# Attention and squared-ReLU FFN in one kernel: the last 64 keys of two pairs of heads, multiplied with their values on quarters of the array

## The chip, the cores and the metric

The kernel runs on one core of a Trainium2 chip. The metric is the device time of one execution in microseconds, less being better. An execution covers the whole program, with the input and output in the chip's memory.

## The reference

Queries and keys are normalised by their root mean square and scaled by a gain; softmax attention follows; the heads are laid side by side and go through a feed-forward network whose activation is the square of a ReLU. All is float32.

```python
# q, k, v: (8, 12, 448, 64); g_q, g_k: (64,); w_in: (768, 2048); w_out: (2048, 768)
def _attn_ref(q, k, v, g_q, g_k):
    def rmsnorm(x, g):
        rms = np.sqrt(np.mean(x * x, axis=-1, keepdims=True) + 1e-06)
        return x / rms * g
    q_n, k_n = (rmsnorm(q, g_q), rmsnorm(k, g_k))
    scores = 1.0 / np.sqrt(q.shape[-1]) * np.matmul(q_n, k_n.transpose(0, 1, 3, 2))
    scores = scores - np.max(scores, axis=-1, keepdims=True)
    attn = np.exp(scores)
    attn = attn / (np.sum(attn, axis=-1, keepdims=True) + 1e-09)
    return np.matmul(attn, v)

x = attn_out.transpose(0, 2, 1, 3).reshape(8 * 448, 12 * 64)
h = np.maximum(x @ w_in, 0.0)
out = h * h @ w_out                      # (3584, 768)
```

## The kernel before

**Pairs and units.** The work of attention goes by pairs of heads: 8 batches of 6 pairs, 48 pairs, numbered i from 0. The two heads of a pair (e = 0 and 1) lie on partitions 0 to 63 and 64 to 127. The feed-forward network goes by units of two batches, 12 pairs each, so there are four units. `ffn(u)` is a Python generator that writes one product of unit u at each step; it works with Strassen-like products (seven in place of eight), whose operands are the forms `T1` to `T4` of x, the sums `S1` to `S4` of the hidden layer and the weights' forms, which are made in the first unit and kept in device memory.

**Order.** The instructions of each engine stand in the order in which the program writes them; nothing reorders them. While the FFN of one unit runs, the attention of the next unit's pairs is put between its products. Pair i is scored in visit i, and its weights meet the values in visit i + 1. `run(until)` writes FFN products up to a given cost, and then a visit is written. `tasks` and `pool_tasks` are queues of small steps for DVE, ACT and POOL that are written one at a time behind the FFN products. Pairs with `whole(i)`, i > 24, have one visit each (`visit_whole`); pairs 13 to 24 have two half visits (`visit_among`); pairs up to 12 come ahead of the FFN (`visit_alone`). So the visits of the second and third unit's pairs, 24 to 47, are with one exception whole visits, 25 to 48.

**Keys.** Of the 448 keys 384 make three slots (m = 0, 1, 2) of 128 keys. The last 64 keys of an even pair and the last 64 of the odd pair after it share one slot, m = `NJ` = 3: the even pair's on rows 0 to 63, the odd pair's on rows 64 to 127. I call two such pairs a couple. Scores stand with the keys on partitions and the 448 queries along the row.

**A whole visit i, in PE's order:**

- `score` (L397) of slots 0 and 1 of pair i: keys times queries, contracted over 64, so that the two heads run on the two halves of the array's rows; into banks 0, 1 (m=0) and 2, 3 (m=1).
- `attend` (L477) of pair i - 1, slot by slot: values times weights, into bank 4, the two heads on the two halves of the array's columns. `forget` releases the weights' tiles, and `weigh` (L405 on ACT) writes the exponentials of slots 0 and 1 of pair i between them, each into a `wT` tile (8 buffers).
- In an even visit `both_denominators` (L516) of the couple before: four 32-column products of the sums with ones, into bank 0, from where DVE's `take_sums` (L549) transposes them.
- `score` and `weigh` of the slots that are left: m=2 in an odd visit (banks 1, 2); m=2 and m=3 in an even one (banks 1, 2 and 3, 0). The m=3 products serve both pairs of the couple: 64 rows by 64 columns each, two heads by two pairs.

For slot `NJ`, `attend` multiplies the whole 128 rows of the shared weights with the tile `lasts[i % 2]`, which holds this pair's last values on its own 64 rows and zeros on the others:

```python
                nc.tensor.matmul(
                    values_bank(i)[ds(e * D, D), :],
                    lhsT=lasts[i % 2][mine, e, :] if m == NJ else values[i][:, m, e, :],
                    rhs=weights[key_of(i, m), e][mine], start=n == 0, stop=n == NJ,
                )
```

An even pair takes this slot last, in the odd visit that follows it; an odd pair takes it first, in the next even visit (`values_of`). `load_v` (L342, L347 on SP) loads a pair's values in its own visit.

**After a visit.** In an odd visit ACT copies bank 4, the even pair's unnormalised values, to its x tile (L1162). POOL adds up the weights of the slots (`add_up`, L424). After an even visit `invert_both` takes reciprocals of the couple's sums and spreads them; POOL multiplies the even pair's x by them (L535), and `finish` multiplies the odd pair's values, out of bank 4, on DVE (L582). Then the x tiles are taken into the forms (L610).

**FFN lines.** L705 is the first product (its PSUM roles are banks 5 to 7, copied by ACT at L712, made into the hidden layer on DVE at L725 and ACT at L726 and L727); POOL makes the hidden sums (L741); L757 and L786 are the second products; DVE adds them up (L827, L803), ACT in the first block (L825, L801). L651 and L656 load the weights' forms.

Of the kernel before, what the change touches and what calls it, by code (L numbers as in the profile page):

```python
# [13 lines left out]
F32 = mybir.dt.float32  # L14
# [3 lines left out]
ALU = mybir.AluOpType  # L18
# [3 lines left out]
P = 128  # L22


NJ = 3
# [198 lines left out]
def program(ctx, tc, rows, v, g, wide, ones, moe_w_in, moe_w_out, out, shift):  # L224

    nc = tc.nc

    B, H, S, D = v.shape
# [21 lines left out]
    lasts = [const.tile([P, 2, D], F32, name=f"lasts{n}") for n in range(2)]  # L250
# [7 lines left out]
    banks = [psum.tile([P, 512], F32, name=f"bank{n}") for n in range(8)]  # L258
# [4 lines left out]
    LASTS = S - NJ * P  # L263
    assert 2 * LASTS == P and LASTS == D and NPAIR % 2 == 0
    values, turned, through = {}, {}, {}
    weights, sums, inverse, xts, forms = {}, {}, {}, {}, {}
    complete = deque()


# [4 lines left out]
    def whole(i):  # L274
        return i > 2 * 2 * NPAIR

    def slots_of(i, n):

        return [m for m in (2 * n, 2 * n + 1) if m < NJ + 1 - i % 2]

    def values_of(i):

        return [NJ, 0, 1, 2] if i % 2 else [0, 1, 2, NJ]

    def key_of(i, m):
        return (i - i % 2, m) if m == NJ and not shift else (i, m)

    def alone(i):

        return pairs[i][0] < 2  # L290
# [47 lines left out]
    def load_v(i):  # L338
        b, c = pairs[i]
        values[i] = io.tile([P, NJ, 2, D], F32, name="vt", tag="vt")  # L340
        for e in range(2):
            nc.sync.dma_start(  # L342
                values[i][:, :, e],
                rows.in_chunks(i, v[b, 2 * c + e, 0 : NJ * P]),
            )
        mine = ds(i % 2 * D, D)
        nc.sync.dma_start(  # L347
            lasts[i % 2][mine],
            v[b, 2 * c : 2 * c + 2, NJ * P : S].rearrange("h p d -> p h d"),
        )  # L350

    def rescale(i, x):
        rows.power(i, x)
# [35 lines left out]
    def score(i, m):  # L389

        scs = banks_of(i, m)
        for p in (i, i + 1) if m == NJ else (i,):
            some = ds(p % 2 * LASTS, LASTS) if m == NJ else ds(0, P)
            keys = ds(m * P, LASTS if m == NJ else P)
            for e, sc in enumerate(scs):
                r = ds(e * D, D)
                nc.tensor.matmul(  # L397
                    sc[some], lhsT=turned[p, 1][r, keys], rhs=turned[p, 0][r, :],
                    start=True, stop=True,
                )  # L400

    def weigh(i, m):

        for e, sc in enumerate(banks_of(i, m)):
            nc.scalar.activation(  # L405
                new_weights((i, m), e), sc, AF.Exp,
                scale=rows.rr[i][:, 1, 2 * m + e : 2 * m + e + 1],
            )

    def additions(i):  # L410

        order = [NJ, 2] if i % 2 else [2, NJ]
        for m in [1] + order:
            for e in range(2):
                pool_tasks.append(lambda m=m, e=e: add_up(i, e, m))

    def add_up(i, e, m):
        if m == 1:
            sums[i, e] = new_sum(i)
            left = weights[(i, 0), e]  # L420
        else:
            left = sums[i, e]
        some = ds(i % 2 * LASTS, LASTS) if m == NJ else ds(0, P)
        nc.gpsimd.tensor_tensor(  # L424
            out=sums[i, e][some], in0=left[some], in1=weights[key_of(i, m), e][some], op=ALU.add
        )

    def new_sum(i):

        if i % 2 == 0 and whole(i + 1):  # L430
            return new_words().bitcast(F32).rearrange("p n w -> p (n w)")[:, 0:S]
        return att.tile([P, S], F32, name="sum", tag="sum", bufs=2)
# [31 lines left out]
    def values_bank(i):  # L464
        return banks[4 + i % 2 if alone(i) else 4][:, 0:S]

    def attend(i, some):

        order = values_of(i)
        for n in some:
            m = order[n]
            mine = ds(i % 2 * LASTS, LASTS) if m == NJ and shift else ds(0, P)
            for e in range(2):
                nc.tensor.matmul(  # L477
                    values_bank(i)[ds(e * D, D), :],
                    lhsT=lasts[i % 2][mine, e, :] if m == NJ else values[i][:, m, e, :],
                    rhs=weights[key_of(i, m), e][mine], start=n == 0, stop=n == NJ,  # L480
                )

    def add_weights(i, some):

        order = values_of(i)
        for n in some:
            m = order[n]
            mine = ds(i % 2 * LASTS, LASTS) if m == NJ and shift else ds(0, P)
            for e in range(2):
                nc.tensor.matmul(  # L490
                    sums_bank(i)[ds(e * D + n % 2 * SIDE, SIDE), :],
                    lhsT=ones_of[i % 2][mine] if m == NJ else ones[:, 0:SIDE],
                    rhs=weights[key_of(i, m), e][mine], start=n < 2, stop=n >= 2,
                )

    def forget(i, some):

        for n in some:
            m = values_of(i)[n]
            if m < NJ or i % 2 or shift:  # L500
                for e in range(2):
                    del weights[key_of(i, m), e]
# [10 lines left out]
    def both_denominators(i):  # L513

        for n in range(4):
            nc.tensor.matmul(  # L516
                sums_bank(i)[ts(n, SIDE), :], lhsT=ones[:, 0:SIDE],
                rhs=sums.pop((i + n // 2, n % 2)), start=True, stop=True,
            )
        take_sums(i)  # L520
# [48 lines left out]
    def new_words():  # L569
        return ffn_p.tile([P, HALF, 2], U32, name="words", tag="words", bufs=3)  # L570
# [4 lines left out]
    def new_x():  # L575
        return ffn_p.tile([P, S], F32, name="xT", tag="xT", bufs=11 * NK - 1)

    def finish(i):

        b, c = pairs[i]  # L580
        xts[b, c] = new_x()
        nc.vector.tensor_tensor(  # L582
            out=xts[b, c], in0=values_bank(i), in1=inverse.pop(i), op=ALU.mult
        )
        leave(i)

    def leave(i):
        b, c = pairs[i]
        for x in range(2):
            del turned[i, x]  # L590
        del values[i]
        if b == 1:
            begin_forms(c)
        elif b % 2 and c >= NK:
            complete.append((b // 2, c - NK))
# [408 lines left out]
    def run_tasks(most):  # L1004
        for some in (tasks, pool_tasks):
            for _ in range(min(len(some), most)):
                some.popleft()()
# [33 lines left out]
    def weigh_slots(i, n):  # L1041
        if not shift:
            for m in slots_of(i, n):
                score(i, m)
                weigh(i, m)
        elif n:
            weigh_shifted(i)

    def attend_all(i):
        slots = range(NJ + 1)  # L1050
        attend(i, slots)
        add_weights(i, slots)
        forget(i, slots)
        take_sums(i)
        invert(i)
        finish(i)

    def visit_alone(i, n):
        step = i * 2 * VISITS + 2 * n
        if n == 0:  # L1060
# [10 lines left out]
            if i and not shift:  # L1071
                attend(i - 1, range(NJ))
# [53 lines left out]
    def prepare(i):  # L1126

        if i > last:
            return
        room = []  # L1130
        tasks.append(
            lambda: room.append(io.tile([P, 4 * P], F32, name="squares", tag="squares", bufs=1))
        )
        for x in range(2):
            tasks.append(lambda x=x: square(i, x, room[0]))
            tasks.append(lambda x=x: rows.add(i, x))
        tasks.append(lambda: pool_tasks.append(lambda: put_in_order(i)))
        if in_blocks(i):
            tasks.append(lambda: load_blocks(i, 1))

    def visit_whole(i):
        run_tasks(len(tasks) + len(pool_tasks))
        if i <= last and not shift:
            for m in slots_of(i, 0):
                score(i, m)
        if shift:
            attend_all(i - 1)
        else:
            for n in range(NJ + 1):
                attend(i - 1, (n,))  # L1150
                forget(i - 1, (n,))
                if i <= last and n < 2:
                    weigh(i, n)
            if i % 2 == 0:
                both_denominators(i - 2)
        if i <= last:
            weigh_slots(i, 1)
            load_v(i)
        if not shift:
            if i % 2:  # L1160
                xts[pairs[i - 1]] = new_x()
                nc.scalar.copy(xts[pairs[i - 1]], values_bank(i - 1))  # L1162
            else:
                tasks.append(lambda: invert_both(i - 2))
            if i <= last:
                additions(i)
        if shift or i % 2:
            prepare(i + 3)
        else:
            tasks.append(lambda: tasks.append(lambda: prepare(i + 3)))  # L1170
# [78 lines left out]
```

## Time and profile before

| | |
|---|---|
| median of 9 runs | 1432.25 us (1431.55 to 1435.97) |
| the profiled execution's own time | 1434.28 us |
| its span in the profile | 1432.9 us |
| PE, matmuls busy | 1407.6 us, 98% |
| DVE, ACT, POOL busy | 659.7, 592.5, 676.2 us |
| DMA queue 1, share of 16 engines | 44.7% |

Busy time is a union of records: PE's matmuls are pipelined and overlap, so a row's mean duration is longer than what a matmul adds to the span. In a row of groups, the numbers after the bar are the group's busy time in microseconds, the mean of one in nanoseconds, the engine's idle time just before, and what ended it. A float32 product appears as two records, one for each pass. In a row of the timeline the first number is the start, the second the time from the first record's start to the last one's end, both in microseconds. The line numbers are those of the kernel before. In the changed kernel the same lines lie lower by 8 to 29.

### The profile page before, as it was taken

The page shows a single profiled execution, that of the slowest core. Times are in us where ns is not written, and L with a number is a line of the kernel's source. Part 1 is how long each engine was busy: PE and PEld are TensorE (multiplying, and loading weights), DVE is VectorE, ACT ScalarE, POOL GpSimd, SP SyncE. Part 2 cuts the span into 40 slices and gives each one's busy share as a digit, 9 for nine tenths or more (in the row PEclk, how much of TensorE's full clock was granted, in tenths as well). Part 3 has the DMA queues.
Part 4 walks back from the last instruction along what each step waited for, and adds up shares of the span by engine and source line. Part 5 has one row for each costly group of instructions (what it writes and reads, how often), then busy time and mean ns, then how long its engine had stood idle before and what let it go on. Part 6 is the DMA issues. An engine that isn't in the chain of part 4 may idle for free.

```text
span 1432.9 us, 15428 instructions
## 1 busy us (share of the span) xinstructions
PE 1407.6 (98%) x4932; PEld 681.7 (48%) x4932; DVE 659.7 (46%) x1233; ACT 592.5 (41%) x1114; POOL 676.2 (47%) x676
## 2 busy tenths in 40 slices
PE   7999999999999999999999999999999999999998
PEld 3333444444444445445454544445454455555554
DVE  5997366877777513324252452224233241132413
ACT  6874566557555244442415234351432303212130
POOL 5667654746556656446445565464462422021110
PEclk9999999999999999999999999999999999999999
DMA  5765346665676663444435454343622232313122
GB/s 138 193 197 154 66 112 177 171 201 141 196 204 200 186 180 95 148 116 125 118 65 175 113 182 128 98 128 77 183 70 89 94 154 78 113 53 127 38 89 80
DMA packets 309279, 188.12 MB, mean 131 GB/s; under 512 B 265796, under 2 KB 293316, under 8 KB 300996
## 3 DMA queue, kind: packets, MB, share of 16 engines
q1 hardware_dynamic: 308896, 186.97, 44.7%
q8 instruction: 41, 0.67, 0.2%
q14 instruction: 50, 0.41, 0.1%
q10 hardware_dynamic: 292, 0.07, 0.0%
HBM read 144.57 MB, written 42.40 MB: 130 GB/s over the span
## 4 chain that ended last, share of the span: by engine, by line
PE 90%; DVE 4%; SPq 2%; DMA 1%; issue 1%; ACT 1%; POOL 1%; DVEq 0%; POOLq 0%; ACTq 0%
PE bank L705 35%; PE bank L786 29%; PE bank L477 9%; PE bank L397 9%; PE bank L757 5%; PE bank L490 1%; PE bank L507 1%; PE bank L516 1%; SPq L157 1%; DVE acc L827 1%; DVE out_sb L946 0%; PE bank L362 0%; SPq L166 0%; ACT wT L405 0%; DMA q_rows<-qk 0%
## 5 line engine op out<-in xcount | busy, mean ns | idle before, releaser
L705 PE MATMUL bank<-xT,in_sb 128*128 128x448 f32 x1344 | 515.4, 542 | 0.0
L705 PEld LDWEIGHTS bank<-xT,in_sb 128*128 128x128 f32 x1344 | 252.4, 190 | 260.4 <-issue 250.7
L827 DVE TENSOR_TENSOR acc<-acc,bank 128x384 f32<-128x384 f32 x324 | 173.8, 550 | 233.4 <-PE bank L786 183.7
L786 PE MATMUL bank<-out_sb,hid 128*128 128x384 f32 x768 | 266.6, 487 | 0.5 <-DVE acc L827 0.5
L725 DVE TENSOR_TENSOR hid<-bank,part 128x448 f32<-128x448 f32 x128 | 76.9, 622 | 329.7 <-PE bank L705 328.3
L405 ACT ACTIVATE wT<-bank,rr 128x448 f32<-128x448 f32 x288 | 161.2, 633 | 121.5 <-PE bank L397 70.3
L786 PE MATMUL bank<-out_sb,sums 128*128 128x384 f32 x576 | 204.0, 490 | 3.4 <-DVE acc L827 3.3
L786 PEld LDWEIGHTS bank<-out_sb,hid 128*128 128x128 f32 x768 | 145.4, 190 | 104.5 <-DVE acc L827 2.5
L202 POOL TENSOR_TENSOR rr<-ms,minus_half 128x8 f32<-128x8 f32 (+1 forms) x96 | 146.2, 1523 | 91.5 <-DVE ms L195 80.5
L741 POOL TENSOR_TENSOR sums<-hid 128x384 f32<-128x384 f32 x32 | 32.2, 1006 | 302.1 <-ACT hid L727 302.1
L397 PE MATMUL bank<-qT,kT 64*128 64x448 f32 (+1 forms) x768 | 164.5, 574 | 1.5 <-DVE qT L370 1.1
L726 ACT ACTIVATE hid<-hid 128x448 f32<-128x448 f32 x128 | 73.3, 572 | 196.5 <-DVE hid L725 196.5
L786 PEld LDWEIGHTS bank<-out_sb,sums 128*128 128x128 f32 x576 | 107.7, 190 | 88.2 <-DVE acc L827 8.4
L712 ACT COPY part<-bank 128x448 f32<-128x448 f32 x128 | 67.7, 529 | 175.5 <-PE bank L705 175.5
L424 POOL TENSOR_TENSOR sum<-sum,wT 128x448 f32<-128x448 f32 (+1 forms) x96 | 110.6, 1173 | 10.9 <-ACT wT L405 8.1
L397 PEld LDWEIGHTS bank<-qT,kT 64*128 64x128 f32 (+1 forms) x768 | 55.8, 174 | 103.9 <-issue 67.4
L477 PE MATMUL bank<-wT,vt 128*64 128x448 f32 x480 | 102.2, 546 | 0.0
L757 PE MATMUL bank<-out_sb,hid 128*128 128x384 f32 x256 | 85.6, 488 | 0.0
L528 POOL COPY few<-few 32x14 f32<-32x14 f32 x48 | 9.0, 188 | 153.3 <-DVE few L526 151.4
L424 POOL TENSOR_TENSOR sum<-wT 128x448 f32<-128x448 f32 x48 | 56.7, 1199 | 50.4 <-ACT wT L405 50.4
L192 DVE TENSOR_REDUCE ms<-squares 128x8 f32<-128x512 f32 (+1 forms) x68 | 41.8, 614 | 77.0 <-ACT squares L179 77.0
L727 ACT ACTIVATE hid<-hid 128x448 f32<-128x448 f32 x128 | 73.8, 577 | 4.1
(96 smaller groups left out, 1280.0 us busy)
## 6 DMA issues: line engine op xcount, KB each, us to landing
out_sb<-out_forms SPq DMA_DIRECT2D x24, 1536.0 KB, 9.9
in_sb<-in_forms SPq DMA_DIRECT2D x24, 1344.0 KB, 5.9
words<-in_moe_w_in_dram SPq DMA_DIRECT2D x32, 384.0 KB, 3.9
words<-in_moe_w_out_dram SPq DMA_DIRECT2D x32, 384.0 KB, 3.9
out_forms<-out_sb SPq DMA_DIRECT2D x8, 1536.0 KB, 7.0
in_forms<-in_sb SPq DMA_DIRECT2D x8, 1344.0 KB, 5.9
qk<-in_q_dram SPq DMA_DIRECT2D x96, 96.0 KB, 3.3
qk<-in_k_dram SPq DMA_DIRECT2D x96, 96.0 KB, 2.6
```

The source lines that it names most:

```text
L202: self.nc.gpsimd.tensor_tensor(out=self.rr[i][:, x, 0 : self.count(i)], in0=ms, in1=self.minus_half.to_broadcast(list(ms.shape)), op=ALU.pow,)
L397: nc.tensor.matmul(sc[some], lhsT=turned[p, 1][r, keys], rhs=turned[p, 0][r, :], start=True, stop=True,)
L405: nc.scalar.activation(new_weights((i, m), e), sc, AF.Exp, scale=rows.rr[i][:, 1, 2 * m + e : 2 * m + e + 1],)
L424: nc.gpsimd.tensor_tensor(out=sums[i, e][some], in0=left[some], in1=weights[key_of(i, m), e][some], op=ALU.add)
L477: nc.tensor.matmul(values_bank(i)[ds(e * D, D), :], lhsT=lasts[i % 2][mine, e, :] if m == NJ else values[i][:, m, e, :], rhs=weights[key_o ...
L705: nc.tensor.matmul(ps, lhsT=w_sb[:, IN.index(left), c, :], rhs=forms[u, c][right], start=first and c == 0, stop=c == NK - 1, skip_group_ch ...
L725: nc.vector.tensor_tensor(out=dst, in0=left, in1=right, op=op)
L726: nc.scalar.activation(dst, dst, AF.Relu)
L727: nc.scalar.activation(dst, dst, AF.Square)
L757: nc.tensor.matmul(ps, lhsT=flat[a][:, t, ds(NT * P, P)], rhs=w_sb[t][:, 2 * a + half, :], start=(a, t) == parts[0], stop=(a, t) == parts[-1],
L786: nc.tensor.matmul(ps, lhsT=lefts[left][:, t, ts(tt, P)], rhs=w_sb[t][:, OUT.index(right), :], start=first and t == 0, stop=t == 1, skip_g ...
L827: nc.vector.tensor_tensor(out=acc, in0=acc, in1=ps, op=ALU.add)
```

## The change

`joint(i)` holds for pairs 24 to 47. For them the slot `NJ` is taken once for a couple, in the odd visit, by `attend_both`: four products of 64 rows by 64 columns, of two heads and two pairs. Those of the even pair add to bank 4, those of the odd pair write bank 0. An odd pair's `attend` has three slots left. ACT copies bank 0 to a tile (`rests`, from the pool `words`, 3 buffers) ahead of the copy of bank 4. `finish` of an odd pair adds that tile to bank 4 on DVE and multiplies by the reciprocals on POOL. The last values of both pairs are loaded in the even visit; in the odd visit the even pair's are loaded once more. The weights of the shared slot are released after POOL's last addition.

```diff
+    def joint(i):
+        return whole(i - i % 2 + 1) and not shift
...
     def values_of(i):
-        return [NJ, 0, 1, 2] if i % 2 else [0, 1, 2, NJ]
+        if i % 2:
+            return [0, 1, 2] if joint(i) else [NJ, 0, 1, 2]
+        return [0, 1, 2, NJ]
...
-        mine = ds(i % 2 * D, D)
-        nc.sync.dma_start(
-            lasts[i % 2][mine],
-            v[b, 2 * c : 2 * c + 2, NJ * P : S].rearrange("h p d -> p h d"),
-        )
+        for odd in range(2):
+            if joint(i) != (i % 2 == odd) or joint(i) and i % 2 == 0:
+                h = 2 * (c - i % 2 + odd)
+                nc.sync.dma_start(
+                    lasts[odd][ds(odd * D, D)],
+                    v[b, h : h + 2, NJ * P : S].rearrange("h p d -> p h d"),
+                )
...
+        if joint(i) and i % 2 and m == NJ:
+            del weights[key_of(i, m), e]
...
             m = order[n]
+            if joint(i) and m == NJ:
+                attend_both(i)
+                continue
...
-                    rhs=weights[key_of(i, m), e][mine], start=n == 0, stop=n == NJ,
+                    rhs=weights[key_of(i, m), e][mine], start=n == 0, stop=n == len(order) - 1,
                 )
+    def attend_both(i):
+        other = banks[0][:, 0:S]
+        for p in (i, i + 1):
+            r = ds(p % 2 * LASTS, LASTS)
+            for e in range(2):
+                nc.tensor.matmul(
+                    (other if p % 2 else values_bank(i))[ds(e * D, D), :],
+                    lhsT=lasts[p % 2][r, e, :], rhs=weights[(i, NJ), e][r],
+                    start=p > i, stop=True,
+                )
+        rests[i + 1] = new_words().bitcast(F32).rearrange("p n w -> p (n w)")[:, 0:S]
...
-        xts[b, c] = new_x()
-        nc.vector.tensor_tensor(
-            out=xts[b, c], in0=values_bank(i), in1=inverse.pop(i), op=ALU.mult
-        )
+        xT = xts[b, c] = new_x()
+        if joint(i):
+            nc.vector.tensor_tensor(out=xT, in0=values_bank(i), in1=rests.pop(i), op=ALU.add)
+            nc.gpsimd.tensor_tensor(out=xT, in0=xT, in1=inverse.pop(i), op=ALU.mult)
+        else:
+            nc.vector.tensor_tensor(out=xT, in0=values_bank(i), in1=inverse.pop(i), op=ALU.mult)
...
-            for n in range(NJ + 1):
+            for n in range(len(values_of(i - 1))):
                 attend(i - 1, (n,))
...
             if i % 2:
+                nc.scalar.copy(rests[i], banks[0][:, 0:S])
                 xts[pairs[i - 1]] = new_x()
                 nc.scalar.copy(xts[pairs[i - 1]], values_bank(i - 1))
```

More of the change, by code (lines that the diff above doesn't have):

```diff
@@ L265, in program @@
     values, turned, through = {}, {}, {}
-    weights, sums, inverse, xts, forms = {}, {}, {}, {}, {}
+    weights, sums, inverse, rests, xts, forms = {}, {}, {}, {}, {}, {}
     complete = deque()
```

## The prediction

> **What bounds the kernel now.** I read the shares of busy time first, then the chain of waits, then the groups by shape, then the timeline of one couple of visits. The first two views:
>
> ```profile
> PE 1407.6 (98%) x4932; PEld 681.7 (48%) x4932; DVE 659.7 (46%) x1233; ACT 592.5 (41%) x1114; POOL 676.2 (47%) x676
> ...
> PE 90%; DVE 4%; SPq 2%; DMA 1%; issue 1%; ACT 1%; POOL 1%; DVEq 0%; POOLq 0%; ACTq 0%
> ```
>
> PE hardly rests and no other engine is busy half the time. So the change is worth what it takes from PE's own row of instructions, less the waits that it puts there. The clock line of the page reads 9 tenths in every slice, so clock plays no part. The groups that the change touches:
>
> ```profile
> L477 PE MATMUL bank<-wT,vt 128*64 128x448 f32 x480 | 102.2, 546 | 0.0
> L477 PE MATMUL bank<-wT,lasts 128*64 128x448 f32 x192 | 46.5, 563 | 2.5 <-DVE xT L582 2.5
> L582 DVE TENSOR_TENSOR xT<-bank,inverse 128x448 f32<-128x448 f32 x36 | 22.3, 620 | 1.1
> L535 POOL TENSOR_TENSOR xT<-xT,inverse 128x448 f32<-128x448 f32 x12 | 14.0, 1167 | 11.4 <-ACT hid L726 10.2 <-DVE inverse L533 1.2
> L1162 ACT COPY xT<-bank 128x448 f32<-128x448 f32 x12 | 6.4, 532 | 0.0
> ```
>
> Of the 192 records on `lasts`, 4 belong to each pair (two heads, two passes of each float32 product). A mean of 546 ns is a latency, since neighbours overlap; prices must come from the distances between starts. First an even visit (number 26), then an odd one (29):
>
> ```profile
> 526.80 0.97 PE L477 MATMUL bank<-wT,lasts 128*64 128x448 f32 x4
> 527.61 2.42 PE L477 MATMUL bank<-wT,vt 128*64 128x448 f32 x12
> 529.96 0.57 PE L516 MATMUL bank<-words,ones 128*32 128x448 f32 x2
> 529.98 0.57 PE L516 MATMUL bank<-sum,ones 128*32 128x448 f32 x2
> 530.36 0.55 PE L516 MATMUL bank<-words,ones 128*32 128x448 f32 x2
> ...
> 530.85 1.97 PE L397 MATMUL bank<-qT,kT 64*128 64x448 f32 x12
> 532.75 0.64 PE L705 MATMUL bank<-xT,in_sb 128*128 128x448 f32 x1
> ```
>
> ```profile
> 612.33 2.48 PE L477 MATMUL bank<-wT,vt 128*64 128x448 f32 x12
> 614.63 0.92 PE L477 MATMUL bank<-wT,lasts 128*64 128x448 f32 x4
> 615.48 1.02 PE L397 MATMUL bank<-qT,kT 64*128 64x448 f32 x4
> 616.44 1.02 PE L705 MATMUL bank<-xT,in_sb 128*128 128x448 f32 x2
> ```
>
> Read the first column. The even visit's four blocks take 529.96 - 526.80 = 3.16 us, the odd one's 615.48 - 612.33 = 3.15. The three `vt` blocks of the odd visit take 614.63 - 612.33 = 2.30; the even visit's first block takes 0.81, which leaves 1.49 for two more: 0.75 each, and 0.05 extra for the first after a change of tile shape. The odd visit's last block takes 0.85, so leaving a shape costs 0.10. In the even visit L397 does both m=2 (64x128 tiles) and m=3 (four 64x64 quarters, 8 records) from 530.85 to 532.75, 1.90 us; m=2 alone takes 616.44 - 615.48 = 0.96 in the odd visit. So four quarters cost 0.94 with both changes of shape. That is the shape the change wants, already in this kernel.
>
> **The change, part by part.** Twelve couples of pairs (24 and 25 up to 46 and 47) are touched.
>
> *Even visits, 26 to 48.* The odd pair's `lasts` block, 4 records, goes. The first `vt` block then pays the 0.05, so the row of blocks falls from 3.16 to 2.30 + 0.10 = 2.40 us: -0.75 us (two-digit rounding aside), twelve times, -9.0 us. What would be late next? L516 needs bank 0 read by the first exponential; in visit 26 that runs from 527.87 for 0.63, ending 528.50, while L516 moves from 529.96 to 529.21. The m=3 quarters need bank 3 (fourth exponential, ends 530.08; quarters move from 531.80 to 531.05) and bank 0 (L549, 0.65 us on DVE, starting 0.22 us after L516's last matmul, which moves with L516). Covers of 0.7 and 1.0 us remain even if ACT gains nothing.
>
> *Odd visits, 25 to 47.* The even pair's `lasts` block of 0.75 us gives way to eight quarter records. By the odd rows: three blocks and a change, 2.40, then quarters at L397's 0.94, then m=2: 3.34 against 3.15, so +0.19 us. Some 0.04 of the 0.94 is a wait for L549 that the new quarters don't have, so +0.15 to +0.19; I take 0.17. The new quarters in bank 0 wait for the first exponential of this visit: ACT begins at 613.33 and ends it at 613.96, the quarters would start at 614.73. Cover 0.77 us. In visit 25 alone the exponentials begin late (499.69) and m=2 already waits for them until 501.41; there the quarters wait too, but behind that same wait, and I charge nothing. Eleven times 0.17 is +1.9 us.
>
> Is one part unseen? L397's quarters are issued with row groups alternating; the new ones name the same rows twice, then the other rows twice, and the first two add into a bank that already holds a sum. From below, column tiles on the same rows do run together: L516 has four records within 0.02 us (529.96, 529.98) and its next pass at 530.36. From above, two by two would add one round of two passes, 0.75. I take the lower end, since L477 and L516 are both of that kind, and keep the upper for a rival.
>
> The Trainium skill, "TensorE: Matmul & The Clock Gate", Part 3 (Packing small matmuls), speaks against that choice: a weight load runs beside matmuls in flight only where it names another row group, and matmuls keep strict order. By it the second quarter of each row group would wait, and the gain would be gone. L516's four starts on the same rows within 0.02 us do not fit it, and I go by them.
>
> *ACT.* Twelve copies of bank 0, like L1162 at 0.53 us, 6.4 us in all, put ahead of L1162:
>
> ```profile
> 617.65 0.53 ACT L1162 COPY xT<-bank 128x448 f32<-128x448 f32 x1
> 619.00 0.53 ACT L712 COPY part<-bank 128x448 f32<-128x448 f32 x1 [0.82 <-PE bank L705]
> ```
>
> ACT then idles 0.82 us until PE has a bank for it, so the copy fits; in the three odd visits where squares (L179) follow instead, they move by 0.53 and the next gap takes it. Without this cover: up to +6.4 us. Bank 0 is next written in the following visit, over 20 us on.
>
> *DVE and POOL.* L582 stays at 0.62 us and adds instead of multiplying. POOL gains a product like L535, 12 x 1.17 = 14.0 us. Behind it on POOL stand the additions L424 and, in four of the twelve even visits, the hidden sums L741, which PE needs:
>
> ```profile
> 539.99 4.39 POOL L424 TENSOR_TENSOR words<-words,wT 128x448 f32<-128x448 f32 x4
> 545.14 1.00 POOL L741 TENSOR_TENSOR sums<-hid 128x384 f32<-128x384 f32 x1 [0.76 <-ACT hid L727]
> ```
>
> The 0.76 us of idling leaves 0.4 us of shift, so the first sum is ready at 546.5, and PE reads it at 549.61 (some 0.75 earlier at most). The product also delays an odd pair's x by 1.17 us. It matters most at the last couple: L582 ends 1161.35, the product 1162.5, L610 on DVE reads it at 1163.48, and the last unit's first L705 is at 1170.38. Hidden. Without cover: up to +14 us.
>
> *SP.* `lasts` is loaded 36 instead of 24 times over these visits: 12 more issues of 0.62 us and 32 KB (landing 2.5 us). The extra load of an odd visit rewrites the even half and so waits on SP for this visit's quarters; behind it stand block loads or `out_sb` loads (in visit 29 it was issued at 616.38, when the quarters would be over). Weights are loaded two steps ahead, 9.9 us to landing. Nothing on PE.
>
> **The sum.** -9.0 + 1.9 = -7.1 us. Against the profiled execution, 1434.28 us (its span of 1432.9 and 1.4 around it), this gives 1427.2. That execution lies 2.03 us above the median of the runs, 1432.25, so the median should come to 1425.2, 0.50% less. A measurement of this kernel can tell about 0.2%, 2.9 us.
>
> **Its own range.** Per couple the odd visit could cost nothing extra (-0.75, so -9.0 and 1423.2) or a second change of shape and a late bank (+0.37, -4.6 and 1427.7).
>
> **The rivals.**
>
> *No gain: quarters two by two.* One more round of 0.75 in each odd visit: +9.0, sum +1.9, 1434.2 us, within 0.2%. For it: same rows twice running. Against: L516 and L477. The same time would come if the exponentials came 1.7 us later in even visits, so that bank 3 held m=3 back: the trace has them 1.7 us early, and the change frees their buffers sooner, not later.
>
> *Slower: quarters one after another.* Place: the quarter block of each odd visit. Price: four products of two passes at 0.375, 3.0 instead of 0.75 us, +2.25 per couple, +27 us; sum +19.9, 1452 us. It decides from the point where that block exceeds 0.94 + 0.59 = 1.53 us, and shows as slower beyond 1.77. For it: that accumulation into bank 4 begins in one shape and ends in another is not seen in this trace. Against: L397's quarters, four at a time.
>
> *Part of the gain.* The ACT copy or the POOL product finds PE waiting in some couples, say 0.3 us in each: +3.6, 1428.8 us.
>
> **How the numbers follow.** The forecast 0.74, part of the gain 0.09, no gain 0.08, slower 0.09. The range of 1423.0 to 1429.3 holds the first two, 0.83, less what lies outside any of these cases. Faster by over 0.2%: 0.82; within 0.2%: 0.09; slower: 0.09.
>
> **What would show it.** Right: in even visits L516 starts 2.40 us after the first `vt` block; in odd visits the quarters start 2.40 us after it and m=2 some 0.9 us later; records on `lasts` fall where couples are, and no new wait appears on PE. Wrong: quarter starts spread over more than one round, m=2 1.7 us or more behind the quarters, or PE idle ahead of L705 and L786 with ACT or POOL named.

## The result, and the profile after

The changed kernel takes 1426.96 us (median of 10 runs, 1424.72 to 1428.52) against 1432.46 us for the kernel before (31 runs): ratio 0.9957, 95% interval 0.9949 to 0.9964, that is 0.43% or 6.2 us less. The ratio is estimated from all the runs, and not the quotient of the two medians, which differ by 5.5 us. Its profiled execution took 1427.44 us with a span of 1425.6 us. In what follows "before" and "after" are the profiled executions of these two kernels.

The page of the changed kernel, shares of busy time and chain of waits:

```profile
PE 1400.7 (98%) x4932; PEld 678.3 (48%) x4932; DVE 660.7 (46%) x1233; ACT 597.5 (42%) x1126; POOL 689.6 (48%) x688
...
PE 92%; DVE 3%; SPq 1%; issue 1%; DMA 1%; ACT 1%; POOL 1%; DVEq 0%; POOLq 0%; ACTq 0%
```

PE has as many records as before and 6.9 us less busy time; ACT and POOL have 12 instructions more each. The same two visits in the timeline of PE, 26 and then 29 (start, time to the last end):

```profile
526.51 2.48 PE L490 MATMUL bank<-wT,vt 128*64 128x448 f32 x12
528.92 0.57 PE L542 MATMUL bank<-words,ones 128*32 128x448 f32 x2
...
529.81 1.97 PE L405 MATMUL bank<-qT,kT 64*128 64x448 f32 x12
531.70 0.64 PE L733 MATMUL bank<-xT,in_sb 128*128 128x448 f32 x1
```

```profile
610.69 2.48 PE L490 MATMUL bank<-wT,vt 128*64 128x448 f32 x12
613.10 0.98 PE L502 MATMUL bank<-wT,lasts 64*64 64x448 f32 x8
614.01 1.02 PE L405 MATMUL bank<-qT,kT 64*128 64x448 f32 x4
614.97 1.02 PE L733 MATMUL bank<-xT,in_sb 128*128 128x448 f32 x2
```

In the even visit L542 comes 528.92 - 526.51 = 2.41 us after the first block, where L516 came 3.16 us after: -0.75. In the odd visit the quarters start 2.41 us after the first block and m=2 another 0.91 us later, 3.32 against 3.15: +0.17. Eight records from first start to last end in 0.98 us are one round of four, two passes deep.

**How to compare two executions here.** The first FFN product, before anything that the change touches, starts at 136.00 us before and at 136.51 after; over all kernels profiled here it lies between 133.46 and 136.85. Another wait, at some 372 us, takes 0.7 us more in some executions than in others. So totals of single executions can't settle differences of 1 or 2 us. I read the stretch from the first FFN product ahead of visit 25 (485.31 before) to the first one behind visit 48 (1149.63 before), which holds all twelve couples. It takes 664.32 us before and 658.24 after: -6.08 us. Both ends come from the timeline of PE.

| kernel | stretch, us | against before | median, us |
|---|---|---|---|
| before | 664.32 | | 1432.46 |
| after | 658.24 | -6.08 | 1426.96 |
| moved_whole_rows | 664.74 | +0.42 | 1433.35 |
| product_on_dve | 657.81 | -6.51 | 1427.11 |
| act_copy_twice | 658.19 | -6.13 | 1426.35 |
| third_slot_on_quarters | 656.00 | -8.32 | 1424.35 |
| whole_visits_on_quarters | 655.10 | -9.22 | 1424.72 |
| all_visits_on_quarters | 655.11 | -9.21 | 1423.81 |
| all_quarters_unit_end_on_dve | 654.37 | -9.95 | 1421.81 |
| sums_first_on_quarters | 654.05 | -10.27 | 1422.11 |

The medians come from three rounds of runs. In the round of moved_whole_rows to third_slot_on_quarters the kernel before had a median of 1434.38 us, in that of the last four 1434.74, where it has 1432.46 in the table. So compare the ratios given below, each against the kernel before of its own round, and not the medians.

**Where the trace and the sum part.** Twelve even visits give -9.0 and eleven odd ones about +1.8, as predicted; that is -7.2. The stretch is 1.1 us longer than this, in one place: the FFN products right behind visit 36, where the second unit's FFN ends (I count them with visit 36). The timelines of PE, before and after:

```profile
828.71 2.42 PE L786 MATMUL bank<-out_sb,sums 128*128 128x384 f32 x7
831.62 1.56 PE L786 MATMUL bank<-out_sb,hid 128*128 128x384 f32 x4 [0.49 <-DVE acc L827]
```

```profile
825.68 1.45 PE L814 MATMUL bank<-out_sb,sums 128*128 128x384 f32 x4
828.76 1.56 PE L814 MATMUL bank<-out_sb,hid 128*128 128x384 f32 x4 [1.62 <-DVE acc L855]
```

The bracket is PE's idle time and who ended it: 0.49 us before, 1.62 after. Just ahead of that DVE makes two forms of x, `t1` and then `t2`, each a subtraction of two x tiles (L610 before, L638 after). DVE before:

```profile
825.64 0.60 DVE L582 TENSOR_TENSOR xT<-bank,inverse 128x448 f32<-128x448 f32 x1
...
827.10 1.44 DVE L610 TENSOR_TENSOR xT<-xT 128x448 f32<-128x448 f32 x1
...
828.93 2.17 DVE L610 TENSOR_TENSOR xT<-xT 128x448 f32<-128x448 f32 x1
831.02 1.01 DVE L827 TENSOR_TENSOR acc<-acc,bank 128x384 f32<-128x384 f32 x2
```

DVE and POOL of the changed kernel:

```profile
821.63 0.60 DVE L609 TENSOR_TENSOR xT<-bank,words 128x448 f32<-128x448 f32 x1
...
823.09 1.51 DVE L638 TENSOR_TENSOR xT<-xT 128x448 f32<-128x448 f32 x1
824.52 0.54 DVE L855 TENSOR_TENSOR acc<-acc,bank 128x384 f32<-128x384 f32 x1
825.62 2.62 DVE L638 TENSOR_TENSOR xT<-xT 128x448 f32<-128x448 f32 x1 [0.56 <-POOL xT L610]
828.16 1.00 DVE L855 TENSOR_TENSOR acc<-acc,bank 128x384 f32<-128x384 f32 x2
```

```profile
821.83 2.22 POOL L432 TENSOR_TENSOR words<-words,wT 128x448 f32<-128x448 f32 x2
824.01 1.57 POOL L610 TENSOR_TENSOR xT<-xT,inverse 128x448 f32<-128x448 f32 x1
825.54 1.12 POOL L432 TENSOR_TENSOR words<-words,wT 64x448 f32<-64x448 f32 x1
826.63 1.12 POOL L638 TENSOR_TENSOR xT<-xT 128x448 f32<-128x448 f32 x1
```

L610 is the new product. DVE had made its input by 822.23, but POOL first finishes two additions and starts it at 824.01. DVE's form t2 (L638) reads the product, waits, and then takes 2.62 us; the FFN additions (L855) that empty PE's banks stand behind it. From the start of the odd pair's x (L582 before, L609 after) to those additions DVE takes 831.02 - 825.64 = 5.38 us before and 828.16 - 821.63 = 6.53 us after. These 1.15 us more are what PE loses: 0.56 is the wait for POOL, 0.45 the longer t2, 0.07 the longer t1.

### The profile page after: what moved, and what is told of

Same layout as the page of the kernel before. It is cut to its first block, busy times and chain, and to the rows that moved or that the text cites. A ratio compares the mean times of both kernels' runs of the same rounds, so it can differ in the third digit from the quotient of the medians.

```text
span 1425.6 us, 15477 instructions
## 1 busy us (share of the span) xinstructions
PE 1400.7 (98%) x4932; PEld 678.3 (48%) x4932; DVE 660.7 (46%) x1233; ACT 597.5 (42%) x1126; POOL 689.6 (48%) x688
## 4 chain that ended last, share of the span: by engine, by line
PE 92%; DVE 3%; SPq 1%; issue 1%; DMA 1%; ACT 1%; POOL 1%; DVEq 0%; POOLq 0%; ACTq 0%
PE bank L733 35%; PE bank L814 29%; PE bank L405 9%; PE bank L490 9%; PE bank L785 5%; PE bank L516 1%; PE bank L502 1%; PE bank L533 1%; PE bank L542 1%; SPq L157 1%; PE bank L370 1%; DVE acc L855 0%; DMA words<-in_moe_w_out_dram 0%; DVE out_sb L974 0%; ACT wT L413 0%
## 5 line engine op out<-in xcount | busy, mean ns | idle before, releaser
L855 DVE TENSOR_TENSOR acc<-acc,bank 128x384 f32<-128x384 f32 x324 | 173.8, 550 | 232.4 <-PE bank L814 185.0
L202 POOL TENSOR_TENSOR rr<-ms,minus_half 128x8 f32<-128x8 f32 (+1 forms) x96 | 146.2, 1523 | 82.9 <-DVE ms L195 71.7
L740 ACT COPY part<-bank 128x448 f32<-128x448 f32 x128 | 67.7, 529 | 170.9 <-PE bank L733 170.9
L432 POOL TENSOR_TENSOR sum<-sum,wT 128x448 f32<-128x448 f32 (+1 forms) x96 | 110.4, 1170 | 10.8 <-ACT wT L413 8.1
L432 POOL TENSOR_TENSOR sum<-wT 128x448 f32<-128x448 f32 x48 | 57.1, 1209 | 49.2 <-ACT wT L413 49.2
```

The source lines that it names most:

```text
L202: self.nc.gpsimd.tensor_tensor(out=self.rr[i][:, x, 0 : self.count(i)], in0=ms, in1=self.minus_half.to_broadcast(list(ms.shape)), op=ALU.pow,)
L432: nc.gpsimd.tensor_tensor(out=sums[i, e][some], in0=left[some], in1=weights[key_of(i, m), e][some], op=ALU.add)
L855: nc.vector.tensor_tensor(out=acc, in0=acc, in1=ps, op=ALU.add)
```

## Experiments

### moved_whole_rows: the block in its new place, but not on quarters

```diff
-                    lhsT=lasts[p % 2][r, e, :], rhs=weights[(i, NJ), e][r],
+                    lhsT=lasts[p % 2][:, e, :], rhs=weights[(i, NJ), e],
```

> The changed kernel, but the four products of a couple's last keys run on all 128 rows (the other pair's rows of the values are zeros), as before; they stay in the odd visit, with bank 0, the ACT copy and the POOL product. Theory (the gain is the packing of four quarters into one round of the array): an even visit still loses its block of 0.75 us, the odd visit gets it, so from visit 25 to visit 48 PE's starts come out level with the kernel before, but for the 1.1 us of waiting at visit 36 that the POOL product makes; 1432.5 to 1434 us, ratio 1.000 to 1.001. In the trace the two blocks of last keys in an odd visit take 1.5 us and a change of shape instead of 0.91. Rival (the gain comes from where the block stands: exponentials and buffers are free sooner, or the odd pair's wait is gone): at least half of the gain stays, 1429 us or less.

1433.35 us, ratio 0.9999 (0.9989 to 1.0009); the stretch +0.42. PE in visit 29:

```profile
609.00 2.48 PE L490 MATMUL bank<-wT,vt 128*64 128x448 f32 x12
611.31 1.67 PE L502 MATMUL bank<-wT,lasts 128*64 128x448 f32 x8
612.91 1.02 PE L405 MATMUL bank<-qT,kT 64*128 64x448 f32 x4
```

The eight records on whole rows take 612.91 - 611.31 = 1.60 us with the change of shape, where the quarters take 0.91. From visit to visit the lead over before goes +0.75, -0.75, with nothing left over except 1.1 us lost in visit 36, and some 0.7 us gained in visit 25, where the wait for the exponentials hides most of the second block. The gain is the packing; the place alone brings nothing.

### act_copy_twice: the cover of the ACT copy

```diff
                 nc.scalar.copy(rests[i], banks[0][:, 0:S])
+                nc.scalar.copy(rests[i], banks[0][:, 0:S])
```

> The changed kernel with the ACT copy of bank 0 made twice in each odd visit, 12 copies of 0.53 us more. Theory (the copy has cover: ACT idles 0.8 us after it and PE needs what follows later still): PE's starts move by under 0.1 us in each odd visit, the time within 0.1% of the changed kernel. Rival (the copy is on the path, and part of what the quarters gain is paid back there): up to 0.5 us more in each odd visit, 6 us in all.

1426.35 us, the stretch 658.19 against 658.24. ACT in visit 29, first of the changed kernel, then with two copies (L1189, L1190) where the change has one:

```profile
616.11 0.53 ACT L1189 COPY words<-bank 128x448 f32<-128x448 f32 x1
616.52 0.55 ACT L1191 COPY xT<-bank 128x448 f32<-128x448 f32 x1
617.52 0.53 ACT L740 COPY part<-bank 128x448 f32<-128x448 f32 x1 [0.45 <-PE bank L733]
```

```profile
613.98 1.16 ACT L413 ACTIVATE wT<-bank,rr 128x448 f32<-128x448 f32 x2 [1.16 <-PE bank L405]
615.03 0.53 ACT L1189 COPY words<-bank 128x448 f32<-128x448 f32 x1
615.59 0.53 ACT L1190 COPY words<-bank 128x448 f32<-128x448 f32 x1
616.02 0.54 ACT L1192 COPY xT<-bank 128x448 f32<-128x448 f32 x1
616.45 0.55 ACT L740 COPY part<-bank 128x448 f32<-128x448 f32 x1
```

The bracket of 0.45 us that L740 has in the changed kernel is gone: ACT is full here. PE still does not wait. The single copy is free, with room for another.

### product_on_dve: the product that PE waited for

```diff
-            nc.gpsimd.tensor_tensor(out=xT, in0=xT, in1=inverse.pop(i), op=ALU.mult)
+            nc.vector.tensor_tensor(out=xT, in0=xT, in1=inverse.pop(i), op=ALU.mult)
```

> The changed kernel with the odd pair's product with the reciprocals on DVE instead of POOL. Theory (in visit 36, the end of the second unit's FFN, DVE's form t2 waits for the POOL product, which stands behind POOL's additions, and PE waits for DVE): PE's gap of 2.11 us at 826 us in the changed kernel falls to about 1.0 as in the kernel before; 1.1 us less than the changed kernel, about 1425.5, the other stages unchanged since 0.6 us more on DVE has cover. Rival (the gap comes from DVE's own slow forms, 2.6 us for t2, whatever made its input): the gap stays or grows, and the time is that of the changed kernel or 1 us more.

1427.11 us, ratio 0.9951 (0.9937 to 0.9964), which does not tell it from the changed kernel; the stretch is 0.43 us shorter. PE in visit 36:

```profile
825.84 1.56 PE L814 MATMUL bank<-out_sb,hid 128*128 128x384 f32 x4 [0.73 <-DVE acc L855]
```

Its idle time there fell from 1.62 to 0.73 us, and visit 36 with it by 0.75 us on balance. (The expectation counts from one matmul's start to the next one's: 2.11 us in the changed kernel, 0.98 before, 1.22 here.) So the product's place on POOL caused most of that wait. It did not fall to 0.49, and 0.35 us was lost again in visit 46, where DVE's transpose of bank 0 began late with DVE idle; why, the trace does not show. The expected 1.1 us was therefore not reached.

### third_slot_on_quarters: one change of shape less

```diff
+            if m == 2 and whole(i) and not shift:
+                for h in range(2):
+                    for e, sc in enumerate(scs):
+                        r = ds(e * D, D)
+                        nc.tensor.matmul(
+                            sc[ds(h * D, D)], lhsT=turned[p, 1][r, ds(m * P + h * D, D)],
+                            rhs=turned[p, 0][r, :], start=True, stop=True,
+                        )
+                continue
```

> The changed kernel with the scores of slot m=2 in visits 25 to 47 written as four products of 64 keys on quarters of the array, next to the quarters that stand beside them in each visit, so that PE changes its tile shape once less in each of these 23 visits. Theory (a change of shape costs 0.10 us to leave and 0.05 to 0.10 to enter, and nothing else of the odd visit's 0.16 is left): in odd visits the stretch from the first quarter of the last keys to the FFN falls from 1.87 to about 1.66 us; in even visits bank 0 is held by DVE's transpose and at most 0.1 us is gained; together 2.5 to 4 us less than the changed kernel, 1423 to 1425 us. Rival (quarters cost more than half-array products beside the change of shape, by their doubled number of instructions): no gain or a loss, 1427 us or more.

1424.35 us, ratio 0.9935 (0.9921 to 0.9949); the stretch is 2.24 us shorter than after. PE in visit 29, then in visit 26:

```profile
611.08 0.98 PE L511 MATMUL bank<-wT,lasts 64*64 64x448 f32 x8
611.88 0.93 PE L407 MATMUL bank<-qT,kT 64*64 64x448 f32 x8
612.74 1.77 PE L742 MATMUL bank<-xT,in_sb 128*128 128x448 f32 x4
```

```profile
527.99 0.98 PE L407 MATMUL bank<-qT,kT 64*64 64x448 f32 x8
528.79 1.17 PE L414 MATMUL bank<-qT,kT 64*64 64x448 f32 x8
529.88 1.02 PE L742 MATMUL bank<-xT,in_sb 128*128 128x448 f32 x2
```

In the odd visit the last keys and m=2 take 612.74 - 611.08 = 1.66 us in place of 1.87: this is 0.20 us in each, and it wipes out the +0.16 that the odd visits cost after the change. In the even visit m=2 and m=3 take 1.89, as before: m=3 (L414) stretches to 1.17 us, waiting for DVE to empty bank 0. The odd visits came as expected; the even ones gained nothing, where up to 0.1 us was allowed, and the total of 2.24 us lies just under the 2.5 to 4 expected.

### whole_visits_on_quarters and all_visits_on_quarters: the other scores too

The condition becomes `m < NJ and whole(i) and not shift`, and then `m < NJ and not shift`.

> As third_slot_on_quarters, and slots m=0 and m=1 of visits 25 to 47 on quarters too. Theory (entering quarters delays the second pass by 0.05 us, entering half arrays by 0.10): 0.05 us less in each of 23 visits, about 1.1 us less than third_slot_on_quarters from visit 25 to 48, so that stretch comes out near -9.4 us against the kernel before. Rival (twice the instructions for the same product cost PE time): the stretch is as long as there or longer.

> As whole_visits_on_quarters, with the scores of slots 0 to 2 on quarters in every visit, those ahead of the FFN and those of the first unit's stretch (visits 0 to 24) too. Theory: in the half visits m=2 stands next to m=3 and saves a change of shape of 0.2 us every second pair, and 0.05 us at each other entry; up to 1.5 us less between 136 us and visit 25. Rival (that stretch is held by DMA, ACT and DVE, as PE's gaps of 1.0 to 1.7 us there show): no change there beyond the spread between executions, which is 3 us by 136 us.

The first: 1424.72 us, ratio 0.9937 (0.9923 to 0.9950); stretch 655.10, 0.90 us less than third_slot_on_quarters, against 1.1 expected. Twice the instructions cost PE nothing that shows. The second: 1423.81 us, ratio 0.9917 (0.9903 to 0.9932). It leaves the stretch alone and shortens what lies ahead of it: from the first FFN product to visit 25 PE takes 1.5 us less than before, expected up to 1.5. Kernels without this edit vary there by more than 1 us on their own (from -0.9 to +0.5), but place by place the starts agree. Of the 35 places there where attention stands between FFN products, 18 are 0.04 us shorter than before and the last is 0.20 us shorter, 0.9 us together, which no kernel without the edit shows. Another 0.67 us falls in one place, at some 265 us, where the kernels without the edit differ by 0.35 us among themselves; that piece is likely, not certain. The 0.2 us expected in every second pair came only once.

### all_quarters_unit_end_on_dve: only where it matters

```diff
-            nc.gpsimd.tensor_tensor(out=xT, in0=xT, in1=inverse.pop(i), op=ALU.mult)
+            engine = nc.vector if i % (2 * NPAIR) == 2 * NPAIR - 1 else nc.gpsimd
+            engine.tensor_tensor(out=xT, in0=xT, in1=inverse.pop(i), op=ALU.mult)
```

> As all_visits_on_quarters, with the odd pair's product on DVE for pairs 35 and 47 alone, the last of each unit, and on POOL for the others. Theory (only there does the POOL product reach PE, through DVE's form t2): PE's gap of 2.1 us in visit 36 falls to 1.2 as in product_on_dve, and the 0.35 us that product_on_dve lost at its visit 46 does not appear: 0.9 us less. Rival (the loss is in DVE's slow forms): the gap stays.

1421.81 us, ratio 0.9914 (0.9899 to 0.9929). The stretch is 0.74 us shorter than without this edit, where 0.9 was expected; the 0.35 us of visit 46 did not come back. PE and DVE in visit 36:

```profile
825.02 1.24 PE L824 MATMUL bank<-out_sb,hid 128*128 128x384 f32 x3 [0.72 <-DVE acc L865]
```

```profile
818.65 0.60 DVE L618 TENSOR_TENSOR xT<-bank,words 128x448 f32<-128x448 f32 x1
819.29 1.18 DVE L620 TENSOR_TENSOR xT<-xT,inverse 128x448 f32<-128x448 f32 x1
...
821.32 0.62 DVE L648 TENSOR_TENSOR xT<-xT 128x448 f32<-128x448 f32 x1
...
822.33 2.17 DVE L648 TENSOR_TENSOR xT<-xT 128x448 f32<-128x448 f32 x1
824.43 1.01 DVE L865 TENSOR_TENSOR acc<-acc,bank 128x384 f32<-128x384 f32 x2
```

The product (L620) is ready 1.9 us before t2 (the second L648) starts. DVE's row takes 824.43 - 818.65 = 5.78 us, 0.40 more than before. t2 takes its 2.17 us as before, so it is not what is left: the product adds 1.18 us to DVE's row, and t1 gives back 0.82 (0.62 us where it took 1.44). By these rows what is left of the wait is the product's own time on DVE. This version beats the changed kernel and the kernel before: its interval lies clear of both.

### sums_first_on_quarters: the couple's sums at the start of the visit

`both_denominators` moves ahead of the scores of an even visit and writes bank 3; otherwise whole_visits_on_quarters with pairs 35 and 47 on DVE.

> As whole_visits_on_quarters, with pairs 35 and 47 on DVE, and the couple's four sums (both_denominators) written at the start of an even visit into bank 3 in place of before m=2 into bank 0. Theory (in even visits the m=3 quarters wait for DVE's transpose of bank 0, which took the gain of the saved change of shape): m=3 then follows m=2 without a wait and an even visit loses another 0.2 us, 2 us in all; the m=1 scores of bank 3 have m=0's 0.75 us as cover for the transpose. Rival (DVE stands behind FFN additions at the start of a visit, so that the transpose comes later and m=1 waits): up to 0.5 us more in each even visit.

1422.11 us, ratio 0.9919 (0.9906 to 0.9933). PE in visit 26:

```profile
524.48 1.90 PE L407 MATMUL bank<-qT,kT 64*64 64x448 f32 x16
526.30 2.48 PE L499 MATMUL bank<-wT,vt 128*64 128x448 f32 x12
528.71 0.98 PE L407 MATMUL bank<-qT,kT 64*64 64x448 f32 x8
529.51 0.93 PE L414 MATMUL bank<-qT,kT 64*64 64x448 f32 x8
530.37 1.02 PE L743 MATMUL bank<-xT,in_sb 128*128 128x448 f32 x2
```

m=2 and m=3 fall to 530.37 - 528.71 = 1.66 us, as the theory said. But the first 16 records take 526.30 - 524.48 = 1.82 us; without this edit they took 1.67 (523.29 to 524.96). The wait for DVE's transpose has moved from bank 0 to bank 3. Some 0.07 to 0.10 us is left in most even visits, where 0.2 was expected, so the theory of the cover was wrong. In visit 36 the rival came true, which makes that visit 0.47 us longer than without this edit. PE and DVE there:

```profile
801.06 2.41 PE L407 MATMUL bank<-qT,kT 64*64 64x448 f32 x16
```

```profile
801.84 0.61 DVE L584 STREAM_TRANSPOSE inverse<-bank 128x448 f32<-128x448 f32 x1
```

DVE first finishes other work and begins the transpose (L584) 0.78 us behind the start of the scores, where it is 0.21 us in visit 26. In all, the stretch is 0.32 us shorter than that of all_quarters_unit_end_on_dve, which has the same edits from visit 25 on but for this one; 2 us was expected.

## Why the prediction was right, and one step that was not

Forecast: 1425.2 us, 0.50% less; measured 1426.96, 0.43% less, interval 0.36 to 0.51. One term was wrong, by 1.1 us of the 7.1; the stated range had room for it.

- *Even visits.* Forecast -0.75 us each, measured -0.75. None of the named covers failed: no wait appeared at L516's or m=3's places.
- *Odd visits.* Forecast +0.15 to +0.19, measured +0.16. Pricing the new quarters by L397's m=3 was sound. In visit 25 the two kernels differ by 0.03 us, as the existing wait there suggested.
- *Four at a time.* The rule of the Trainium skill ("TensorE: Matmul & The Clock Gate", Part 3) on weight loads and row groups, as the prediction read it, would have had the quarters in two rounds. The eight records span 0.98 us in the trace of after, one round, so the measurement decides against it for column tiles on the same rows. The rivals with two or four rounds fall with this.
- *ACT.* Free, shown with twice the load.
- *POOL: the step that failed.* The prediction set the product to nothing ("It matters most at the last couple ... Hidden."). The last couple is not where it matters: in visit 48 PE ran as forecast. It matters in visit 36, where forms of two columns of x, the additions of the next couple and the FFN's last block share POOL and DVE. There it cost 1.13 us of waiting, and product_on_dve and all_quarters_unit_end_on_dve got 0.75 of it back. The rest is the product's own time on DVE, some 0.4 us net. The working looked at the time when data would be ready, and not at the queue that stood in front of the product, nor at how long DVE's forms take while POOL is busy.
- *The sum.* -7.1 less the 1.1 of visit 36 is -6.0; the stretch shows -6.08.

## What to carry to other kernels

Two half-empty products that were padded with zeros can be packed as quarters; here the results of the two row groups go to different banks, and one bank for both was not tried. The price is found from starts in a place of the same kernel that already has that tile shape. Put products of the same shape beside each other: here a saved change of shape was worth 0.2 us, more than the new one had cost, but only where no PSUM bank was late. When work goes to an engine with "time to spare", look for the visit in which that engine's queue is longest, at the ends of units, and follow the reader behind it.

## What the hardware showed unexpectedly

DVE's subtraction of two SBUF tiles (128x448, float32: L610 before, L638 after) occurs 24 times in each of the ten traces. Leaving aside POOL's small instructions of L202 (128x6 and 128x8), its time goes with what POOL does when it starts:

- In 84 of the 240 cases POOL has no elementwise instruction beside it: 0.61 to 0.63 us.
- In 30 it begins 0.04 to 0.05 us ahead of one on POOL: 0.62 to 0.63 us too.
- In 126 it begins while one runs on POOL. 116 of these end 0.48 to 0.55 us after the end of that instruction, however much of it was left, and take up to 1.54 us.
- The other ten are t2 of visit 36, one in each trace. They end 0.48 or 0.49 us after the end of the next instruction on POOL, and take 2.17 to 2.63 us. In the rows of after, t2 begins at 825.62, just behind the start of L432 on POOL; the L638 that follows there ends at 827.75, and t2 at 828.24.

So DVE's subtraction waits until POOL's instruction is over. The product on POOL therefore cost twice in visit 36: t2 waited for it, and then began at the start of another POOL instruction, where before it had begun halfway through one. Why t2 waits for two and the others for one, the traces do not show.
